# Attention in 36 slots and experts with gathers two jobs ahead: every engine put into written order

## The chip, the cores and the metric

The kernel runs on one core of one Trainium2 chip. The metric is the device time of one execution in microseconds (us), lower is better. A core has five engines with a queue each: TensorE (PE in the profile; its weight loads are PEld), VectorE (DVE), ScalarE (ACT), GpSimd (POOL) and SyncE (SP, which here only issues transfers). Each engine takes its own instructions in order and waits for others by semaphores.

## The reference

Eight batches, eight heads, 576 tokens, head dimension 64. Attention without softmax, an RMS norm per head, then a switch layer: each of the 4608 tokens goes to one of eight experts.

```python
kv  = einsum('bhsd,bhse->bhde', k, v)
o   = einsum('bhsd,bhde->bhse', q, kv)
o   = o / sqrt(mean(o*o, -1) + 1e-6) * g_norm
x   = o.transpose(0, 2, 1, 3).reshape(4608, 512)
logits = x @ w_gate                       # [4608, 8]
e   = argmax(logits, 1)
p   = softmax(logits)[n, e]
out = p * (relu(x @ w1[e]) @ w2[e])       # w1 [8,512,1024], w2 [8,1024,512]
```

All inputs are float32; the experts' weights and rows are used as float16.

## The kernel before

**Attention.** Four pairs of batches `P`, nine tiles of 128 tokens in each: four of the first batch, four of the second, and one with the last 64 tokens of both. `load_qkv` (L149) loads k, v or q of one batch into a 1 MB buffer `ld`, of which there are four; `load_q` copies q by heads into `qp` on POOL (L162). `kv_stage` (L174) forms k^T v of a batch: 80 matmuls into `kvp` (L187), copies to `kvs` (L194), transposes `kvtp` (L197), a copy `kvt` (L199), the product with the gate weights `kgp` (L202), a copy (L205). `x_tile` (L208) does one tile: transposes `qtp` (L212), copy `qts` (L214), `op` = q k^T v with the logits beside it (L219; two PSUM buffers), then the norm chain: `sq` on ACT (L230), `ms` on DVE (L235), `lnt` and `rinv` on ACT (L237, L239), the normalised rows `xg` and logits `lr` on DVE (L241, L247). `route` (L254) takes the tiles of a pair together (the last pair in four and five): `lg` and some fifteen small DVE instructions choose the expert, matmuls `pp` count ranks, and POOL scatters each tile's rows to `xs_scratch` in DRAM, sorted by expert (L305).

**Experts.** After counts and a table for left-over rows (L372 to L425), one job per expert plus one for rows beyond five tiles of an expert ("left", one tile here). A job gathers five tiles from `xs_scratch` on POOL (L496), transposes them (`xp`, L441, copy `xt`, L444), computes the row numbers `idx` (L446), `hp` = x w1 with a Relu copy `ht` on ACT (L462, L469), `yp` = h w2 (L478), scales to `ys` on DVE (L483), and POOL scatters to the output (L486). `load_w` loads w1 in float32 to the one buffer `wst` (SP, L127), scales it by g on POOL to `w1e` (L130), and loads w2 with a cast on POOL's queue (`w2e`, L133); four buffers of each.

**Order.** The program is traced as written, and the framework's scheduler then orders the instructions of each engine by its own costs; it may move work of one part between that of another. Only `issue_after` holds some scaling behind the scatters. In the expert loop the gathers of job n+1 are written ahead of `ffn_1` of job n.

Of the kernel before, what the change touches and what calls it, by code (L numbers as in the profile page):

```python
# [13 lines left out]
I32 = mybir.dt.int32  # L14
# [14 lines left out]
def kernel(  # L29
# [42 lines left out]
    for P in range(4):  # L72
# [44 lines left out]
        P_const.tile([128, RW], F16, tag=f"xe{n}", name=f"xe{n}") for n in range(2 * CT + 2)  # L117
# [4 lines left out]
    def load_w(e, after=None):  # L122
        e = e if isinstance(e, bass.DynSlice) else slice(e, e + 1)
        w1e = P_w.tile([128, 4, F], F16, tag="w1e", bufs=4, name="w1e")
        w2e = P_w.tile([128, 8, D], F16, tag="w2e", bufs=4, name="w2e")
        st = P_w.tile([128, 4, F], F32, tag="wst", bufs=1, name="wst")
        nc.sync.dma_start(st, moe_w1[e, :, :].rearrange("o (t p) f -> p (o t) f", p=128))  # L127
        with tc.issue_after(after) if after is not None else nullcontext():
            for kk in range(4):
                nc.gpsimd.tensor_scalar(  # L130
                    w1e[:, kk, :], st[:, kk, :], g2, 1.0, op0=ALU.mult, op1=ALU.mult
                )
            nc.gpsimd.dma_start(  # L133
                w2e, moe_w2[e, :, :].rearrange("o (t p) d -> p (o t) d", p=128)
            )
        return w1e, w2e

    weights = {}

    with (  # L140
        tc.tile_pool(name="pattn", bufs=1) as PA,
# [14 lines left out]
        def load_q(b):  # L156

            t = load_qkv(q, b)
            qp = PA.tile([128, 4, 8, 64], F32, tag="qp", bufs=2, name="qp")
            tv = t.rearrange("p h (j d) -> p h j d", j=4)  # L160
            for j in range(4):
                nc.gpsimd.tensor_copy(qp[:, j, :, :], tv[:, :, j, :])  # L162
            return qp

        def load_rem(src, b0, tag, bufs):
            t = PA.tile([128, 8, 64], F32, tag=tag, bufs=bufs, name=tag)
# [7 lines left out]
        def kv_stage(b, kb, vb, kr, vr):  # L174
            kvp = PSA.tile([128, 4, 64], F32, tag="kvp", bufs=1, name="kvp")
            r0 = 64 * (b % 2)
            for i in range(4):
                for j in range(5):
                    for hh in range(2):
                        h = 2 * i + hh  # L180
                        if j < 4:
                            lhs = kb[:, h, 64 * j:64 * j + 64]
                            rhs = vb[:, h, 64 * j:64 * j + 64]
                        else:
                            lhs = kr[r0:r0 + 64, h, :]
                            rhs = vr[r0:r0 + 64, h, :]
                        nc.tensor.matmul(  # L187
                            kvp[64 * hh:64 * hh + 64, i, :], lhs, rhs,
                            start=(j == 0), stop=(j == 4),
                        )  # L190
            kvs = kvs_bufs[b % 4]
            for hh in range(2):
                ps = slice(64 * hh, 64 * hh + 64)
                nc.vector.tensor_copy(kvs[ps, :, 64 * hh:64 * hh + 64], kvp[ps, :, :])  # L194
            kvtp = PSA.tile([128, 4, 128], F32, tag="misc", bufs=1, name="kvtp")
            for i in range(4):
                nc.tensor.transpose(kvtp[:, i, :], kvs[:, i, 0:128], ident)  # L197
            kvt = PA.tile([128, 4, 128], F32, tag="kvt", bufs=1, name="kvt")
            nc.scalar.copy(kvt, kvtp)  # L199
            kgp = PSA.tile([128, 4, 16], F32, tag="misc", bufs=1, name="kgp")  # L200
            for i in range(4):
                nc.tensor.matmul(  # L202
                    kgp[:, i, :], kvt[:, i, :], gw[:, i, :, :], start=True, stop=True
                )
            nc.vector.tensor_copy(kvs[:, :, 128:144], kgp)  # L205
            return kvs

        def x_tile(qsrc, parts, xg, lr, t):  # L208

            qtp = PSA.tile([128, 4, 128], F32, tag="qtp", bufs=2, name="qtp")  # L210
            for i in range(4):
                nc.tensor.transpose(qtp[:, i, :], qsrc(i), ident)  # L212
            qts = PA.tile([128, 4, 128], F32, tag="qts", bufs=2, name="qts")
            nc.scalar.copy(qts, qtp)  # L214
            op = PSA.tile([128, 2, 512], F32, tag="op", bufs=2, name="op")
            for i in range(4):
                c0 = (i % 2) * 144
                for c, kvs in parts:
                    nc.tensor.matmul(  # L219
                        op[c, i // 2, c0:c0 + 144],  # L220
                        qts[:, i, c],
                        kvs[:, i, :],
                        start=True,
                        stop=True,
                    )
            oc = op[:, :, 0:288].rearrange("p c (i n) -> p c i n", n=144)
# [9 lines left out]
            lnt = PA.tile([128, 8], F32, tag="lnt", bufs=3, name="lnt")  # L236
            nc.scalar.activation(lnt, ms, ACTF.Ln, scale=1.0 / 64.0, bias=epsb)  # L237
            rinv = PA.tile([128, 8], F32, tag="rinv", bufs=3, name="rinv")
            nc.scalar.activation(rinv, lnt, ACTF.Exp, scale=-0.5)  # L239
            r4 = rinv.rearrange("p (c i h) -> p c i h", c=2, i=2)  # L240
            nc.vector.tensor_tensor(  # L241
                xg[:, t, 0:512].rearrange("p (c i h n) -> p c i h n", c=2, i=2, h=2),
                ox,
                _bc(r4, 4, 64),
                op=ALU.mult,
            )
            nc.vector.tensor_tensor(  # L247
                lr[:, t, :, :].rearrange("p (c i h) n -> p c i h n", c=2, i=2),
                ol,
                _bc(r4, 4, 8),  # L250
                op=ALU.mult,
            )

        def route(g0, G, xg, lr, tile0):  # L254
            lg = PA.tile([128, G, 8], F32, tag="lg", bufs=2, name="lg")
            nc.vector.reduce_sum(lg, lr[:, g0:g0 + G, :, :].transpose([0, 1, 3, 2]), axis=AXX)
            mx = PA.tile([128, G], F32, tag="mx", bufs=2, name="mx")
            nc.vector.tensor_reduce(mx, lg, axis=AXX, op=ALU.max)
            dl = PA.tile([128, G, 8], F32, tag="dl", bufs=2, name="dl")
            nc.vector.tensor_tensor(dl, lg, _bc(mx, 2, 8), op=ALU.subtract)  # L260

            cd = PA.tile([128, G, 8], F32, tag="cd", bufs=2, name="cd")
            nc.vector.scalar_tensor_tensor(
                out=cd, in0=dl, scalar=0.0, in1=_bc(rev8, 1, G),
                op0=ALU.is_ge, op1=ALU.mult,
            )
            m2 = PA.tile([128, G], F32, tag="m2", bufs=2, name="m2")
            nc.vector.tensor_reduce(m2, cd, axis=AXX, op=ALU.max)
# [324 lines left out]
```

## Time and profile before

| | us |
|---|---|
| median of 3 runs | 422.68 (421.56 to 424.37) |
| the profiled execution | 424.92 |
| its span in the profile | 423.1 |
| busy in the span: PE, DVE, ACT, POOL | 299.4, 143.6, 118.5, 194.0 |
| first stage, to the last scatter of rows | 0 to 201 |
| experts, first `hp` to last `yp` | 213.4 to 413.9 |

The profile's page splits the span into 40 slices with the busy tenths of each engine; the trace can be asked for the busy time of any stretch, for groups of instructions by line, for the instructions in order of time, and for the chain of waits: the work that ended last, followed back from each step to what released it. "PEclk" is TensorE's granted clock as a share of 2.4 GHz.

### The profile page before, as it was taken

To read this page: it belongs to the slowest core of one execution; us is meant where nothing else is said; L and a number is where in the kernel's file an instruction comes from. 1 tells how busy PE (TensorE), PEld (TensorE's weight loads), DVE (VectorE), ACT (ScalarE), POOL (GpSimd) and SP (SyncE) were. 2 spreads that over 40 slices of the span, in tenths; PEclk is the share of its full clock that TensorE was granted. 3 is DMA by queue.
4 is the path that set the end of the run, shared out by engine and by line. 5 is a ranking of instruction groups with operands and counts; after the bars stand their busy time and mean duration, and the time that the engine had idled before them with its cause. 6 is when DMAs were issued, how large, how long until landed. Compare 5 with 4: busy or idle time off the path is not lost.

```text
span 423.1 us, 5972 instructions
## 1 busy us (share of the span) xinstructions
PE 299.4 (71%) x2278; PEld 211.3 (50%) x2278; DVE 143.6 (34%) x370; ACT 118.5 (28%) x294; POOL 194.0 (46%) x216
## 2 busy tenths in 40 slices
PE   0789777845695468740196958879598696979991
PEld 0587666744584457640063534545345354445750
DVE  0134645371246415458213304233141331313321
ACT  1034514430335014340041140422405014041520
POOL 7220238307640371524874673747646472543221
PEclk9999977985699658875586997989989699889997
DMA  8995989987999299151288586566776347231111
GB/s 229 254 308 132 242 305 325 233 223 198 335 281 231 78 324 248 50 200 50 64 246 225 194 156 237 143 153 254 131 267 144 63 138 124 76 108 75 42 52 67
DMA packets 59725, 76.20 MB, mean 180 GB/s; under 512 B 16429, under 2 KB 50478, under 8 KB 59696
## 3 DMA queue, kind: packets, MB, share of 16 engines
q1 hardware_dynamic: 43360, 47.42, 37.2%
q0 software_dynamic: 16336, 28.40, 27.5%
q8 instruction: 18, 0.29, 0.3%
q14 instruction: 11, 0.09, 0.1%
HBM read 71.70 MB, written 15.50 MB: 206 GB/s over the span
## 4 chain that ended last, share of the span: by engine, by line
PE 33%; issue 20%; DMA 16%; POOL 10%; DVE 8%; ACT 6%; SPq 2%; another core or an unknown queue 1%; POOLq 1%; DVEq 0%
PE op L219 11%; PE yp L478 7%; DMA xe<-xs_scratch,rowi 6%; DMA out_dram<-ys,idx 5%; PE kvp L187 5%; POOL out_dram L486 3%; POOL xe L496 3%; PE kgp L202 3%; PE hp L462 3%; ACT sq L230 2%; PE qtp L212 2%; DMA wst<-in_moe_w_dram 2%; POOL w1e L130 2%; ACT qts L214 2%; PE kvtp L197 2%
## 5 line engine op out<-in xcount | busy, mean ns | idle before, releaser
L469 ACT ACTIVATE ht<-hp 128x320 f16<-128x320 f32 (+1 forms) x136 | 56.5, 428 | 156.5 <-PE hp L462 91.4
L478 PE MATMUL yp<-w2e,ht 128*128 128x512 f16 x328 | 85.4, 413 | 0.0
L462 PE MATMUL hp<-xt,w1e 128*128 128x320 f16 (+1 forms) x544 | 77.6, 300 | 10.3 <-ACT ht L469 8.7
L486 POOL DMA_INDIRECT out_dram<-ys,idx x41 | 42.0, 1024 | 73.9 <-DVE ys L483 66.2
L305 POOL DMA_INDIRECT xs_scratch<-xg,sli x36 | 35.3, 981 | 79.4 <-DVE sli L303 57.3
L462 PEld LDWEIGHTS <-w1e 128*128 128x128 f16 x544 | 52.9, 99 | 34.9 <-issue 13.2
L219 PE MATMUL op<-kvs,qts 128*128 128x144 f32 (+1 forms) x320 | 51.8, 340 | 21.2 <-DVE lr L247 13.4
L219 PEld LDWEIGHTS op<-kvs,qts 128*128 128x128 f32 (+1 forms) x320 | 47.0, 222 | 25.1 <-ACT rinv L239 14.3
L478 PEld LDWEIGHTS <-ht 128*128 128x128 f16 x328 | 34.0, 106 | 38.6 <-issue 9.2
L130 POOL TENSOR_SCALAR w1e<-wst,g 128x1024 f16<-128x1024 f32 x36 | 39.8, 1116 | 19.1 <-issue 8.6
L496 POOL DMA_INDIRECT xe<-xs_scratch,rowi x40 | 41.1, 1027 | 12.1 <-issue 11.6
L441 PE MATMUL xp<-ch,xe 128*128 128x128 f16 x164 | 19.7, 267 | 37.8 <-DMA xe<-xs_scratch,rowi 19.5
L446 DVE SCALAR_TENSOR_TENSOR idx<-xe,valid,bigm 128x1 int32<-128x1 int32 x40 | 12.0, 305 | 98.2 <-DMA xe<-xs_scratch,rowi 95.3
L235 DVE TENSOR_REDUCE ms<-sq 128x8 f32<-128x512 f32 x36 | 24.7, 686 | 58.7 <-ACT sq L230 56.2
L483 DVE TENSOR_SCALAR ys<-yp,xe 128x512 f32<-128x512 f32 x41 | 30.7, 749 | 40.7 <-PE yp L478 39.6
L441 PEld LDWEIGHTS <-xe 128*128 128x128 f16 x164 | 14.9, 119 | 46.0 <-issue 23.4
L162 POOL COPY qp<-ld 128x512 f32<-128x512 f32 x32 | 18.3, 620 | 38.0 <-DMA ld<-in_q_dram 38.0
L230 ACT ACTIVATE sq<-op 128x512 f32<-128x512 f32 x36 | 21.5, 598 | 46.8 <-PE op L219 45.1
L187 PE MATMUL kvp<-ld 128*64 128x64 f32 x512 | 26.9, 256 | 10.5 <-DMA ld<-in_v_dram 10.5
L187 PEld LDWEIGHTS kvp<-ld 128*64 128x64 f32 x512 | 22.0, 163 | 13.6 <-issue 10.9
L214 ACT COPY qts<-qtp 128x512 f32<-128x512 f32 x36 | 20.8, 582 | 26.2 <-PE qtp L212 26.2
L212 PE MATMUL qtp<-cf,qp 128*128 128x128 f32 x128 | 21.4, 307 | 7.3 <-issue 6.6
(87 smaller groups left out, 213.3 us busy)
## 6 DMA issues: line engine op xcount, KB each, us to landing
wst<-in_moe_w_dram SPq DMA_DIRECT2D x9, 2048.0 KB, 12.2
w2e<-in_moe_w_dram POOLq DMA_DIRECT2D x9, 1024.0 KB
ld<-in_k_dram SPq DMA_DIRECT2D x8, 1024.0 KB, 7.6
ld<-in_v_dram SPq DMA_DIRECT2D x8, 1024.0 KB, 7.9
ld<-in_q_dram SPq DMA_DIRECT2D x8, 1024.0 KB, 11.0
kr<-in_k_dram SPq DMA_DIRECT2D x8, 128.0 KB, 9.6
vr<-in_v_dram SPq DMA_DIRECT2D x8, 128.0 KB, 7.2
qr<-in_q_dram SPq DMA_DIRECT2D x8, 128.0 KB, 9.8
```

What stands on the lines that cost most here:

```text
L130: nc.gpsimd.tensor_scalar(w1e[:, kk, :], st[:, kk, :], g2, 1.0, op0=ALU.mult, op1=ALU.mult)
L187: nc.tensor.matmul(kvp[64 * hh:64 * hh + 64, i, :], lhs, rhs, start=(j == 0), stop=(j == 4),)
L219: nc.tensor.matmul(op[c, i // 2, c0:c0 + 144], qts[:, i, c], kvs[:, i, :], start=True, stop=True,)
L230: nc.scalar.activation(sq.rearrange("p (c i h) n -> p c i (h n)", c=2, i=2), oc[:, :, :, 0:128], ACTF.Square,)
L305: sent = nc.gpsimd.indirect_dma_start(out=xs_views[tile0 + g0 + t], out_offset=IndirectOffsetOnAxis(ap=sli[:, t:t + 1], axis=0), in_=xg[:, ...
L441: nc.tensor.transpose(xp[:, c, :], xe[t][:, c * 128:(c + 1) * 128], ident16)
L462: nc.tensor.matmul(hp, w1e[:, kk, f * 128:(f + 1) * 128], xt[:, kk, ws * wd:(ws + 1) * wd], start=(kk == 0), stop=(kk == 3),)
L469: nc.scalar.activation(ht[:, f, ws * wd:(ws + 1) * wd], hp, ACTF.Relu)
L478: nc.tensor.matmul(yp, ht[:, f, t * 128:(t + 1) * 128], w2e[:, f, :], start=(f == 0), stop=(f == 7),)
L483: nc.vector.tensor_scalar(ys, yp, xe[t][:, 514:516].bitcast(F32), None, op0=ALU.mult)
L486: nc.gpsimd.indirect_dma_start(out=views[t], out_offset=IndirectOffsetOnAxis(ap=idx[:, t:t + 1], axis=0), in_=ys, in_offset=None, bounds_c ...
L496: nc.gpsimd.indirect_dma_start(out=xe.bitcast(I32), out_offset=None, in_=xs.ap(), in_offset=IndirectOffsetOnAxis(ap=rows, axis=0), bounds_ ...
```

## The change

Both stages are put under `tc.manual_schedule` with all five engines, so that each engine gets its instructions in the order in which they are written.

- Attention is 36 slots, one per tile. Slot s has `x_mm(s)` (`op`), `x_qt(s+2)` (transposes two tiles ahead), the norm chain, and lists of other work: `mid`, `late`, `last`. k^T v of the next batch is put in parts into the four or five slots ahead of its first tile; routing is split in `first`, `ranks` and `send`, in the last slot of a group and the one after it. The last pair is routed in 4, 3 and 2 tiles.
- `ld` has six buffers for four; a batch is loaded two batches ahead. `xe` has sixteen for twelve: three sets of five and one.
- Weights: three buffers each for four. W[0] and W[1] are scaled on POOL during attention, the other seven on VectorE inside the jobs. `stage` (w1 to `wst`) of W[n+3] is issued in job n after the scaling of W[n+2], `second` (w2) of W[n+3] at the end of job n.
- In job n the gathers of job n+2 are issued first; the transposes of job n+1 (`flip`) stand among the second half of the `hp` groups.

```diff
-            t = PA.tile([128, 8, 256], F32, tag="ld", bufs=4, name="ld")
+            t = PA.tile([128, 8, 256], F32, tag="ld", bufs=6, name="ld")
...
+        first_slot = [9 * (b // 2) + 4 * (b % 2) for b in range(B)]
+        for b in range(1, B):
+            f = first_slot[b]
+            n = 4 if b % 2 else 5
+            plan = [[0, 1], [2, 3]] if n == 4 else [[0], [1, 2], [3]]
+            for m, ii in enumerate(plan):
+                for i in ii:
+                    at(late, f - n + m, kv_mm, b, i)
+            at(last, f - 3, kv_copy, b)
+            at(late, f - 2, kv_t, b)
+            at(mid, f - 1, kv_gate, b)
+            for j in range(4):
+                at(last, f - 4 + j // 2, heads, b, j)
+            if b + 2 < B:
+                at(last, f - 2, load_batch, b + 2)
+        for P, g0, G in [(0, 0, 9), (1, 0, 9), (2, 0, 9), (3, 0, 4), (3, 4, 3)]:
+            rt = Route(P, g0, G)
+            s = 9 * P + g0 + G - 1
+            at(last, s, rt.first)
+            at(late, s + 1, rt.ranks)
+            at(last, s + 1, rt.send)
+        at(last, first_slot[4] - 2, W[0].stage)
+        at(last, first_slot[6] - 2, W[0].second)
+        for kk in range(4):
+            at(last, 23 + kk // 2, W[0].scale, nc.gpsimd, kk)
+        at(last, 25, W[1].stage)
+        for kk in range(4):
+            at(last, 32 + kk // 2, W[1].scale, nc.gpsimd, kk)
+        at(last, 33, W[2].stage)
...
+        load_batch(0)
...
+        for j in range(4):
+            heads(0, j)
+        for t in xe_bufs:
+            nc.gpsimd.memset(t, 0.0)
...
+        for s in range(36):
+            op = x_mm(s)
+            for fn in mid[s]:
+                fn()
+            if s + 2 < 36:
+                qt = x_qt(s + 2)
+            rest = x_norm(s, op)
+            if s + 2 < 36:
+                x_qs(s + 2, qt)
+            for fn in late[s]:
+                fn()
+            rest()
+            for fn in last[s]:
+                fn()
+        rt = Route(3, 7, 2)
+        rt.first()
+        rt.ranks()
+        rt.send()
...
+            rows(0)
+            W[1].second()
+            rows(1)
+            W[2].second()
+            for t in range(CT):
+                jobs[0].flip(t)
+            for n in range(len(order)):
+                job = jobs[n]
+                if n == 4:
+                    jobs[7] = left_over(0, 3 * CT, out_views[E * CT])
+                    W[7] = jobs[7].w
+                nxt = jobs[n + 1] if n + 1 < len(order) else None
+                rows(n + 2)
+                flips = list(range(nxt.nt)) if nxt is not None else []
+                for ws in range(job.halves):
+                    for f in range(8):
+                        job.one(ws, f)
+                        if ws == job.halves - 1 and f >= 2 and flips:
+                            nxt.flip(flips.pop(0))
+                        if ws == (n == 0) and f % 2 == 1 and n + 2 < len(order):
+                            W[n + 2].scale(nc.vector, f // 2)
+                            if f == 7 and n + 3 < len(order):
+                                W[n + 3].stage()
+                for t in range(job.nt):
+                    job.two(t)
+                if n + 3 < len(order):
+                    W[n + 3].second()
```

The functions that the slots and jobs call hold the instructions of before: `kv_mm`, `kv_copy`, `kv_t` and `kv_gate` are the parts of `kv_stage`, `one` and `two` those of `ffn_1` and `ffn_2`. `x_norm` issues `sq` and `ms` and returns `rest`, which issues `lnt`, `rinv`, `lr` and `xg`. In it `lr` now stands ahead of `xg`; in `Route`, `ex`, `se` and the two writes into `xg` move from `first` to `ranks`.

## Rows read from the trace of the kernel before

**Rows 1.** The page's 40 slices: tenths of the transfer engines' busy share.
```profile
DMA  8995989987999299151288586566776347231111
```

**Rows 2.** Busy time by stretch, attention: stretch, length, PE, PEld, DVE, ACT, POOL, clock, transfer share, GB/s.
```profile
0.00:114.00 114.00, 75.78 (x740) 66.10 (x741) 41.24 (x112) 33.97 (x84) 45.58 (x69) 0.87 0.92 252
100.00:125.00 25.00, 17.11 (x160) 15.42 (x161) 6.92 (x15) 8.35 (x20) 15.63 (x19) 0.73 1.08 306
```

**Rows 3.** Instructions in order of time at the seam: start, us, engine, line, operation.
```profile
191.23 0.72 DVE L256 TENSOR_REDUCE lg<-lr 128x40 f32<-128x320 f32 x1
...
213.39 9.99 PE L462 MATMUL hp<-xt,w1e 128*128 128x320 f16 x64
```

**Rows 4.** Busy time by stretch, two expert jobs (columns as in rows 2).
```profile
229.10:255.50 26.40, 20.86 (x126) 12.17 (x125) 6.75 (x15) 6.78 (x16) 15.74 (x15) 0.89 0.70 186
...
281.40:306.80 25.40, 19.98 (x123) 11.69 (x121) 6.64 (x14) 6.79 (x16) 16.10 (x16) 0.95 0.72 195
```

**Rows 5.** The chain of waits, at the seam and between two jobs: start, us, what.
```profile
200.41 2.53 DMA xs_scratch<-xg,sli
...
244.20 0.97 POOL w2e L133
...
246.84 7.54 DMA xe<-xs_scratch,rowi
...
255.15 0.59 PE xp L441 x4
```

**Rows 6.** Instructions in order of time, TensorE in the last job.
```profile
396.41 8.86 PE L462 MATMUL hp<-xt,w1e 128*128 128x320 f16 x64
...
405.11 8.80 PE L478 MATMUL yp<-w2e,ht 128*128 128x512 f16 x40
```

**Rows 7.** The chain of waits, TensorE's pieces in attention (x16: two tiles).
```profile
24.25 3.95 PE op L219 x16
...
74.99 1.02 PE qtp L212 x8
...
116.16 2.20 PE op L219 x16
118.36 3.53 PE kvp L187 x80
...
124.16 1.08 PE kgp L202 x8
```

**Rows 8.** Instructions in order of time, the norm chain of one tile alone.
```profile
50.51 0.60 ACT L230 ACTIVATE sq<-op 128x512 f32<-128x512 f32 x1 [1.54 <-PE op L219]
51.14 0.69 DVE L235 TENSOR_REDUCE ms<-sq 128x8 f32<-128x512 f32 x1 [1.28 <-ACT sq L230]
...
53.05 0.21 DVE L247 TENSOR_TENSOR lr<-op,rinv 128x64 f32<-128x64 f32 x1
```

**Rows 9.** Instructions in order of time: first and last of VectorE's routing of nine tiles.
```profile
91.82 1.18 DVE L256 TENSOR_REDUCE lg<-lr 128x72 f32<-128x576 f32 x1
...
95.72 0.17 DVE L303 CAST sli<-sl 128x9 int32<-128x9 f32 x1
```

**Rows 10.** Groups by line and form: count, busy us, mean ns, idle before them.
```profile
L194 DVE COPY kvs<-kvp 64x256 f32<-64x256 f32 x16 | 6.8, 422 | 14.8 <-PE kvp L187 8.6 <-remote 6.0
L391 DVE TENSOR_SCALAR thr<-cf 128x256 f32<-128x256 f32 x1 | 0.3, 286 | 0.0
...
L305 POOL DMA_INDIRECT xs_scratch<-xg,sli x36 | 35.3, 981 | 79.4 <-DVE sli L303 57.3 <-DVE bigm L380 12.7 <-issue 8.8
```

**Rows 11.** Instructions in order of time: `idx` beside a scaling and beside a gather's issue.
```profile
211.29 1.13 POOL L130 TENSOR_SCALAR w1e<-wst,g 128x1024 f16<-128x1024 f32 x1
211.68 0.76 DVE L446 SCALAR_TENSOR_TENSOR idx<-xe,valid,bigm 128x1 int32<-128x1 int32 x1 [0.62 <-DMA xe<-xs_scratch,rowi]
...
237.87 1.02 POOL L496 DMA_INDIRECT xe<-xs_scratch,rowi  x1 [0.30 <-issue]
238.06 0.22 DVE L446 SCALAR_TENSOR_TENSOR idx<-xe,valid,bigm 128x1 int32<-128x1 int32 x1 [1.02 <-DMA xe<-xs_scratch,rowi]
```

More of the change, by code (lines that the diff above doesn't have):

```diff
@@ L116, with __init__, stage, scale @@
     xe_bufs = [
-        P_const.tile([128, RW], F16, tag=f"xe{n}", name=f"xe{n}") for n in range(2 * CT + 2)
+        P_const.tile([128, RW], F16, tag=f"xe{n}", name=f"xe{n}") for n in range(3 * CT + 1)
     ]
     tabi = P_const.tile([128, 2, 32], I32, tag="tabi")
[L122 to L132, printed above, removed]
+    class Weights:
+        def __init__(self, e):
+            self.e = e if isinstance(e, bass.DynSlice) else slice(e, e + 1)
+        def stage(self):
+            self.st = P_w.tile([128, 4, F], F32, tag="wst", bufs=1, name="wst")
+            nc.sync.dma_start(
+                self.st, moe_w1[self.e, :, :].rearrange("o (t p) f -> p (o t) f", p=128)
+            )
+        def scale(self, eng, kk):
+            if kk == 0:
+                self.w1 = P_w.tile([128, 4, F], F16, tag="w1e", bufs=3, name="w1e")
+            eng.tensor_scalar(
+                self.w1[:, kk, :], self.st[:, kk, :], g2, 1.0, op0=ALU.mult, op1=ALU.mult
+            )
+        def second(self):
+            self.w2 = P_w.tile([128, 8, D], F16, tag="w2e", bufs=3, name="w2e")
             nc.gpsimd.dma_start(
-                w2e, moe_w2[e, :, :].rearrange("o (t p) d -> p (o t) d", p=128)
+                self.w2, moe_w2[self.e, :, :].rearrange("o (t p) d -> p (o t) d", p=128)
             )
-        return w1e, w2e
-    weights = {}
+    ENG = mybir.EngineType
+    by_hand = {ENG.PE, ENG.Activation, ENG.DVE, ENG.Pool, ENG.SP}
+    order = list(range(E - 1)) + ["left", E - 1]
+    W = [Weights(e) if e != "left" else None for e in order]
     with (
+        tc.manual_schedule(engines=by_hand),
         tc.tile_pool(name="pattn", bufs=1) as PA,
@@ L154, in load_qkv, with load_rem @@
             return t
[L156 to L166, printed above, removed]
+        def load_rem(src, b0, tag):
+            t = PA.tile([128, 8, 64], F32, tag=tag, bufs=2, name=tag)
             for bb in range(2):
@@ L172, in load_rem @@
             return t
-        def kv_stage(b, kb, vb, kr, vr):
-            kvp = PSA.tile([128, 4, 64], F32, tag="kvp", bufs=1, name="kvp")
-            r0 = 64 * (b % 2)
[L177 to L191, printed above, removed]
+        ld, rem, qp, kvst = {}, {}, {}, {}
@@ new lines, with at @@
+        first_slot = [9 * (b // 2) + 4 * (b % 2) for b in range(B)]
+        mid = {s: [] for s in range(-4, 36)}
+        late = {s: [] for s in range(-4, 36)}
+        last = {s: [] for s in range(-4, 36)}
+        def at(where, s, fn, *args):
+            where[s].append(lambda: fn(*args))
+        for b in range(1, B):
[12 more added lines that the diff above has]
+                at(last, f - 2, load_batch, b + 2)
@@ L522, in left_over_load @@
             )
-            return [gather(xe_bufs[t0], gi)], w, okm, bgm
-        def load_x(e):
-            return [
-                gather(xe_bufs[(e % 2) * CT + t], rowi[:, e, t:t + 1])
-                for t in range(CT)
-            ]
-        def job(e):
-            if e == "left":
-                xe, w, okm, bgm = left
-                return xe, w, okm, bgm, [out_views[E * CT]]
-            return (rows[e], weights[e], valid[:, e, :], bigm[:, e, :],
-                    out_views[e * CT:(e + 1) * CT])
@@ L560 @@
             with tc.For_i(1, nov) as t:
-                xe, w, okm, bgm = left_over_load(t, 2 * CT + 1)
-                xt, idx = ffn_x(xe, okm, bgm)
-                ht = ffn_1(xt, 1, w[0])
-                ffn_2(xe, ht, idx, w[1], [out_views[E * CT + 1]])
+                job = left_over(t, 3 * CT, out_views[E * CT + 1])
+                job.w.stage()
+                for kk in range(4):
+                    job.w.scale(nc.vector, kk)
+                job.w.second()
+                job.flip(0)
+                for f in range(8):
+                    job.one(0, f)
+                job.two(0)
 _INS = ['q', 'k', 'v', 'g_norm', 'moe_w_gate', 'moe_w1', 'moe_w2']
```

568 lines of the change are left out of this document (305 added, 263 removed).

## The prediction

> **What bounds the kernel now.** I read the slices of the page first, then the busy time by stretch, then the chain of waits in each stage.
>
> The slices (10.6 us each) show the transfers busy at 0.7 or more in 14 of the first 16, at 0.1 to 0.5 in the four after them, then mostly at 0.5 to 0.8 up to the 30th [rows 1]. The first stage, attention and routing, moved 252 GB/s over its first 114 us at a transfer share of 0.92, while TensorE was busy for 75.8 of these 114 us [rows 2]. So attention runs near its transfers, and TensorE is not its bound: its mean granted clock there is 0.87, from 100 to 125 only 0.73, which means that part of it runs at 1.2 GHz.
>
> Between attention and experts lies a seam: from the last `lg` at 191.23 to the first `hp` at 213.39 are 22.2 us [rows 3].
>
> In the expert stage a job of five tiles takes some 26 us, with TensorE busy for 20 to 21 of them at a clock of 0.89 to 0.95 [rows 4]. The chain shows why: the last gather for the next job is issued behind `w2e` on POOL's queue and lands 7.54 us after its issue; then the transposes start from idle, and `xp` takes 0.59 us a tile [rows 5]. The last job, which waits for no gather, takes 17.5 us from its first `hp` to the end of its last `yp` [rows 6].
>
> **The change, stage by stage.** *Start.* The loads of batch 0 keep their order on SP, so the first `op` stays at 24 us [rows 7]. Six `ld` buffers in place of four let batch 1 be issued whole; the clearing of 16 `xe` buffers moves behind the first `heads` copies, where POOL has nothing due. Cost 0.
>
> *Slots 0 to 26.* TensorE at full clock, per tile: `op` 2.20/2 = 1.10 and `qtp` 1.02/2 = 0.51, so 1.61; per batch: `kvp` 3.53, `kgp` 1.08 and `kvtp`, four transposes as in `qtp`, 0.51, so 5.12 [rows 7]. Nine tiles with two batches: 9 x 1.61 + 2 x 5.12 = 24.7 us. VectorE with ScalarE: from the start of `ms` to the end of `lr` 51.14 to 53.26 = 2.12 us, with `lnt` and `rinv` of ScalarE between; the next `sq` fits under `xg` and `lr` [rows 8]. Routing nine tiles takes 91.82 to 95.89 = 4.1 us of VectorE [rows 9], the copies of a batch 2 x 0.42 and a smaller one, about 1.1 [rows 10]. Nine slots: 9 x 2.12 + 4.1 + 2 x 1.1 = 25.4 us. The two sums are nearly equal, but their peaks fall into different slots, and every engine is now in order. On TensorE a slot with two of the four `kvp` parts takes 1.61 + 1.77 = 3.4 (two such, beside the one that shares with `ranks`), with one part 2.5 (two), with `kvtp` 2.1 (two), with `kgp` 2.7; on VectorE the slot of `first` takes 2.12 + 2.5 = 4.6, that of `ranks` and `send` 4.0. The larger in each slot, over nine: 4.6 + 4.0 + 2 x 3.4 + 2 x 2.5 + 2 x 2.1 + 2.7 = 27.3; with waits between engines I take 28. Then 27 slots end at 24 + 3 x 28 = 108 us.
>
> Transfers up to k and v of batch 7: seven batches of 3.54 MB, 2.36 MB of the last, 2.1 MB of W[0] and 2.4 MB of scatters = 31.7 MB. At the old rate of 252 GB/s that is 126 us, at 306, the best 25 us stretch, 104 [rows 2]. I take 252/0.92 = 274 GB/s, thus 116 us, since with six buffers a batch is always queued. `kvp` stands ahead of the next tile on TensorE, so a late k or v stops it. Behind the nine scatters of `send` on POOL, 9 x (0.98 + some 0.30 between) = 11.5 us [rows 10], stand the `heads` copies 2 and 3 of the next batch; they are due four slots, some 12 us, later. For such waits 3 us: slot 27 starts at 119.
>
> *Slots 27 to 35.* No next batch after slot 30, but two more routing parts of 3.3 to 4.1 us. The larger in each slot: 4.0 + 3.4 + 2.1 + 4.0 + 3.8 + 2.1 + 4.0 + 3.7 + 2.1 = 29 us. The last tile is normalised at 148.
>
> *Seam.* Two tiles are left to route: 3.3 us of VectorE (4.1 less 0.8 of the shorter `lg`), 0.3, two scatters 1.3 apart, 2.5 until the second lands, five gathers 5.2 to the last issue, 2.5 to land, 0.6 to `hp` = 15.7, say 16 for 22.2 [rows 3, 5]. The left-over table, some 25 instructions of VectorE of at most 0.29 [rows 10], so up to 7 us, hides under scatters and gathers; without that cover it is added. First `hp` at 164.
>
> *Experts.* A job at full clock is 17.5 plus five tiles of transposes, between 5 x 0.59/2 = 1.5 and nothing (they overlap `hp`); I take 1.2: 18.7 us. Gathers two jobs ahead are issued some 18 us before they are read, which covers the 7.54. What is late next is transfers: 0.70 x 26.4 = 18.5 and 0.72 x 25.4 = 18.3 us of them per job [rows 4], 98% of 18.7. There is one `wst`, so `stage` of W[n+3] waits for the scalings of W[n+2]; these stand ahead of the flips on VectorE, so a late `wst` stops `xt` and `ys` and through them TensorE. I allow 1.1 us in jobs 1 to 5, and 3 us in job 0, whose flips read rows gathered behind W[1].second. Scaling moves from POOL to VectorE for seven weights. The trace has no such instruction: it takes at least 0.29, the row of 256 columns, and at most four times that, 1.15 [rows 10]; I take 0.7. Four add 2.8 us (1.2 to 4.6) to VectorE's 6.8 of 26.4 [rows 4]: hidden. Sum: 21.7 + 5 x 19.8 + 18.7 + 4 (left: eight `yp`, 32 short `hp`) + 17.5 = 161. Bounds: 150 without the allowances, and 178 with 22.4 us in jobs 0 to 5 (18.4 us of transfers at a share of 0.82, midway between 0.72 and 0.92).
>
> *Port.* `idx` takes 0.22 us while POOL issues a gather, but took 0.76 while POOL scaled `w1e`, and ended with it at 212.4 [rows 11]: the two engines can shut each other out, and the issue of a gather did not do so. By these rows the scaling on VectorE costs nothing on the path. The Trainium skill (SBUF — State Buffer, section "SBUF: two separate sides") goes further: a VectorE instruction in a two-port mode and a GpSimd one exclude each other for their whole length, and GpSimd cannot write the descriptors of its DMAs meanwhile. The trace agrees with the lock; no row here shows it on descriptors.
>
> *Tail.* From the end of the last `yp`, 413.9, to the end of the span 9.2 us [rows 6]; they stay.
>
> **Sum.** 24 + 95 + 29 + 16 + 161 + 9.2 = 334.2 us of span, where before has 423.1. The profiled execution's own time is 1.8 us above its span, 424.9, so 336.0; the median of the runs shown, 422.7, is 2.2 below that execution. I predict 334.
>
> **The rivals.**
> 1. *Attention keeps its old transfer rate.* For it: a share of 0.92 leaves little to fill. Against: after slice 16 the transfers are half idle while attention still computes [rows 1]. Slot 27 at 129: 344.
> 2. *Experts bound by transfers*, 22.4 us a job, as two more `w2e` fall into the first jobs. For it: 18.4 us of transfers per job. Against: stretches above 0.9 exist [rows 2]. 334 + 17 = 351.
> 3. *The attention order changes nothing*: its bound is elsewhere, and the trace has `kvp` between tiles now. Only seam and jobs gain: 213.4 - 6 + 161 + 9.2 - 0.4 = 377.
> 4. *The written order serialises a slot*, each waiting for the end of the one before: 1.61 + 0.60 for `sq` [rows 8] + 2.12 + 5.12/4.5 + 4.1/9 = 5.9 us, 36 slots 214, `hp` at 254, in all 424; with TensorE at half clock 2.7 more a slot, 521. I put it at 470; it decides from 5.9 us a slot. Against: transposes are written two slots ahead, and `op` has two buffers. This is the side slower than before.
> 5. *The port holds up both engines*: each of 28 scalings waits for an issue of 1.0 us or makes one wait, none hidden: 334 + 28 = 362. For it the 0.76, against it the 0.22. It is what the page above would do here.
>
> **How the numbers follow.** Forecast 0.60, rivals 1 to 5: 0.15, 0.13, 0.06, 0.03, 0.03. All bounds at their low end (compute's 108 hides the 104; 27 for the last slots) give 24 + 84 + 27 + 16 + 150 + 9.2 - 0.4 = 310, rivals 1 and 2 together 361. The forecast's own range is half way to these, 322 to 347. The range from 314 to 360 leaves out rivals 3, 4 and most of 5, and some 0.06 beside. Faster by over 1%, about what a measurement of this kernel can tell: 0.96, all but rival 4 and 0.01 for causes I do not see; slower by over 1%: 0.02; within 1%: 0.02.
>
> **What would show it.** First `op` near 24, slot 27 near 119, first `hp` near 164 and jobs near 19.8 show the terms right one by one; a clock of 1.0 through the experts shows that the gaps are gone. TensorE waiting for `ld` before slot 27 is rival 1; VectorE waiting for `wst` rival 2; POOL issues above 1.03 us beside a scaling rival 5; slots near 6 us rival 4. The prediction is wrong if slots are bound by a wait that I priced at 0.7 us per nine slots, as ScalarE's copy of `kvt` in the middle of a norm chain, or if shares near 1 don't last.

## The result and the profile after

The changed kernel takes 350.95 us (median of 4 runs, 348.39 to 352.36), the kernel before 422.74 beside it: a ratio of 0.829, 95% interval 0.824 to 0.835. The profiled execution took 351.07 us with a span of 349.3, where the kernel before has 423.1. Some kernels below also ran in a slower state, over 1.5% above their fastest run; ratios are those of the faster runs alone.

The profile page's slices come first: clock and transfers, 8.7 us to a slice.

```profile
PEclk9999999859996999675559999999998999999996
DMA  7999999994999772017179879698696969793021
```

Transfers are at 0.9 or more in most of the first 13 slices, where [rows 1] already had 0.8 and 0.9. What is new stands behind them: from the 21st to the 36th slice transfers are at 0.6 to 0.9, in seven of the sixteen at 0.9, where before they went along at 0.5 to 0.8 and lower, and the clock is at 0.9 or more from the 22nd slice on, but for one slice and the last. The same stretches as in [rows 2], and two expert jobs as in [rows 4] (columns as there):

```profile
0.00:114.00 114.00, 84.24 (x942) 73.67 (x942) 49.19 (x126) 44.11 (x107) 46.77 (x75) 0.93 1.00 290
100.00:125.00 25.00, 20.37 (x216) 17.50 (x217) 11.62 (x25) 11.35 (x29) 15.43 (x19) 0.86 0.96 318
191.53:211.50 19.97, 19.43 (x129) 11.69 (x128) 11.45 (x25) 7.81 (x19) 9.60 (x10) 1.00 0.86 236
228.00:247.00 19.00, 18.39 (x124) 11.09 (x121) 8.15 (x17) 6.99 (x16) 9.61 (x11) 1.00 0.88 258
```

In these two jobs TensorE is now busy for 97% of the time at full clock, where [rows 4] had 79% at 0.89 to 0.95. In the attention it is busy for 84 of 114 us, where [rows 2] had 76. The milestones, in order of time (start, us, engine, line, operation): slot 27, the last `lg`, the first `hp`, the fifth and sixth job's `hp`, the last `yp`.

```profile
127.13 1.22 PE L281 MATMUL op<-kvs,qts 128*128 128x144 f32 x8
...
162.21 0.37 DVE L329 TENSOR_REDUCE lg<-lr 128x16 f32<-128x128 f32 x1
...
178.72 8.35 PE L590 MATMUL hp<-xt,w1e 128*128 128x320 f16 x44
...
258.55 6.14 PE L590 MATMUL hp<-xt,w1e 128*128 128x320 f16 x44
...
281.17 6.14 PE L590 MATMUL hp<-xt,w1e 128*128 128x320 f16 x44
...
331.93 8.80 PE L604 MATMUL yp<-w2e,ht 128*128 128x512 f16 x40
```

Against [rows 3] and [rows 6] the 73.8 us of span divide like this: up to the last `lg` 191.23 - 162.21 = 29.0; the seam, last `lg` to first `hp`, 22.2 - 16.5 = 5.7; the experts, first `hp` to the end of the last `yp`, 200.5 - 162.0 = 38.5; the tail 0.6. Against the forecast:

| term | forecast | profile after | late by |
|---|---|---|---|
| slot 27 starts | 119 | 127.1 | 8.1 |
| slots 27 to 35 (last tile) | 29 (148) | 35.1 (162.2) | 6.1 |
| seam | 16 | 16.5 | 0.5 |
| experts | 161 | 162.0 | 1.0 |
| tail | 9.2 | 8.6 | -0.6 |

So 14.2 of the 15.1 us of span that the forecast misses lie in the attention. Two losses are plain in the trace. The first is a stretch in which ScalarE and VectorE sit idle although the results they need of TensorE have long been there. Instructions in order of time; `[..]` is the idle time before one and what ended it ("remote": nothing that the profile knows):

```profile
60.95 1.15 PE L281 MATMUL op<-kvs,qts 128*128 128x144 f32 x8
...
64.47 1.07 PE L241 MATMUL kgp<-gw,kvt 128*128 128x16 f32 x8 [2.38 <-issue]
...
65.39 0.63 PE L263 MATMUL qtp<-cf,qp 128*128 128x128 f32 x4
...
68.10 0.60 ACT L297 ACTIVATE sq<-op 128x512 f32<-128x512 f32 x1 [3.24 <-remote]
...
70.99 0.23 DVE L244 COPY kvs<-kgp 128x64 f32<-128x64 f32 x1 [5.28 <-remote]
...
71.27 2.29 PE L281 MATMUL op<-kvs,qts 128*128 128x144 f32 x8 [5.25 <-DVE kvs L244]
```

`kgp` is complete at 65.5 and its copy starts at 70.99. The same comes at 104.6 (3.43 us idle before it) and 137.5 (2.07). All three begin inside a closed series of nine scatters on GpSimd, issued one behind another (57.9 to 69.1, 96.0 to 107.1, 130.3 to 141.4). Behind the third, TensorE also waits 2.94 us for `qp`. The second loss is this pair, at the end of attention:

```profile
151.49 4.84 DVE L335 TENSOR_TENSOR dl<-lg,mx 128x24 f32<-128x24 f32 x1
...
151.90 4.41 POOL L135 TENSOR_SCALAR w1e<-wst,g 128x1024 f16<-128x1024 f32 x4
...
157.12 0.18 PE L355 MATMUL pp<-cs,ch 128*128 128x24 f16 x1 [6.94 <-DVE cs L347]
```

A subtraction of 24 columns, which takes 0.17 to 0.48 us in the other parts, takes 4.84 us and ends at 156.33, as GpSimd's four scalings of W[1] end at 156.31.

### The profile page after: what moved, and what is told of

It is laid out like the page before. It is cut to its first block, busy times and chain, and to the rows that moved or that the text cites. A ratio compares the mean times of both kernels' runs of the same rounds, so it can differ in the third digit from the quotient of the medians.

```text
span 349.3 us, 5957 instructions
## 1 busy us (share of the span) xinstructions
PE 272.6 (78%) x2279; PEld 195.1 (56%) x2279; DVE 165.0 (47%) x414; ACT 121.7 (35%) x295; POOL 164.6 (47%) x192
## 4 chain that ended last, share of the span: by engine, by line
PE 26%; DMA 26%; DVE 13%; POOL 12%; issue 12%; SPq 4%; another core or an unknown queue 2%; ACT 2%; POOLq 1%; DVEq 0%
DMA w2e<-in_moe_w_dram 12%; DMA out_dram<-ys,idx 9%; PE hp L590 7%; PE yp L604 7%; POOL xs_scratch L389 5%; PE op L281 5%; DMA ld<-in_v_dram 3%; PE kvp L219 3%; POOL xe L543 2%; POOL out_dram L612 2%; SPq L170 2%; DVE xg L314 2%; DVE ms L302 2%; PE qtp L263 2%
## 5 line engine op out<-in xcount | busy, mean ns | idle before, releaser
L590 PE MATMUL hp<-xt,w1e 128*128 128x320 f16 (+1 forms) x544 | 82.0, 302 | 1.2 <-ACT ht L597 1.2
L604 PE MATMUL yp<-w2e,ht 128*128 128x512 f16 x328 | 72.3, 379 | 0.0
L590 PEld LDWEIGHTS <-w1e 128*128 128x128 f16 x544 | 52.3, 100 | 21.3 <-issue 1.3
L281 PE MATMUL op<-kvs,qts 128*128 128x144 f32 (+1 forms) x320 | 50.8, 327 | 12.1 <-DVE kvs L244 7.6
L604 PEld LDWEIGHTS <-ht 128*128 128x128 f16 x328 | 32.1, 98 | 37.1
L281 PEld LDWEIGHTS op<-kvs,qts 128*128 128x128 f32 (+1 forms) x320 | 42.6, 203 | 15.2 <-DVE kvs L244 8.2
L200 POOL COPY qp<-ld 128x512 f32<-128x512 f32 x32 | 18.4, 614 | 42.8 <-DMA ld<-in_q_dram 42.8
L297 ACT ACTIVATE sq<-op 128x512 f32<-128x512 f32 x36 | 21.5, 596 | 35.7 <-PE op L281 23.7
L219 PE MATMUL kvp<-ld 128*64 128x64 f32 x512 | 24.5, 245 | 10.6 <-DMA ld<-in_v_dram 10.6
L571 PE MATMUL xp<-ch,xe 128*128 128x128 f16 x164 | 17.5, 235 | 16.0 <-DMA xe<-xs_scratch,rowi 10.0
L219 PEld LDWEIGHTS kvp<-ld 128*64 128x64 f32 x512 | 19.9, 153 | 15.0 <-issue 13.9
L574 DVE COPY xt<-xp 128x512 f16<-128x512 f16 x41 | 17.2, 418 | 18.9 <-PE xp L571 16.3
L571 PEld LDWEIGHTS <-xe 128*128 128x128 f16 x164 | 13.1, 105 | 20.8 <-DMA xe<-xs_scratch,rowi 11.6
L314 DVE TENSOR_TENSOR xg<-op,rinv 128x512 f16<-128x512 f32 x36 | 24.5, 682 | 0.2
```

Source lines behind the costliest of these rows:

```text
L219: nc.tensor.matmul(kvp[64 * hh:64 * hh + 64, i, :], lhs, rhs, start=(j == 0), stop=(j == 4),)
L281: nc.tensor.matmul(op[c, i // 2, c0:c0 + 144], qts[s][:, i, c], kvs[:, i, :], start=True, stop=True,)
L314: nc.vector.tensor_tensor(xg[:, r, 0:512].rearrange("p (c i h n) -> p c i h n", c=2, i=2, h=2), ox, _bc(r4, 4, 64), op=ALU.mult,)
L571: nc.tensor.transpose(xp[:, c, :], xe[t][:, c * 128:(c + 1) * 128], ident16)
L590: nc.tensor.matmul(hp, self.w.w1[:, kk, f * 128:(f + 1) * 128], self.xt[:, kk, ws * wd:(ws + 1) * wd], start=(kk == 0), stop=(kk == 3),)
L604: nc.tensor.matmul(yp, self.ht[:, f, t * 128:(t + 1) * 128], self.w.w2[:, f, :], start=(f == 0), stop=(f == 7),)
```

## The experiments

Each kernel is the changed one with the edit shown. They ran on three chips (experiments 1 to 4, then 5, 6, 7 and 9, then 8, 10, 11 and 12), each beside the kernel before, so ratios to it are compared, and medians only on one chip.

**1. The q copies ahead of the scatters.**

```
-                at(last, f - 4 + j // 2, heads, b, j)
+                at(last, f - 4 + (j // 2 if b % 2 == 0 else 0), heads, b, j)
```

> The four q copies of an odd batch are all written ahead of the nine scatters of the part before, instead of two ahead and two behind. Theory (GpSimd's written order delays the copies): the 2.94 us that TensorE waits for qp at 142 us goes, and so does the 0.6 us at 107.7, since the copies no longer stand behind 11.4 us of scatters; time 347 us, first hp 3 to 4 us earlier. Rival (the wait only shows what something else would hold): the 142 us wait turns into another wait of the same length, 350 to 351 us. The idle stretches of VectorE before the copy of the gated k^T v at 65.7, 101 and 135 us should stay under both.

Measured: one run of 347.29 us and three of 353.4 to 354.2, before 425.09. They spread too far to say whether the edit gains. In the profile, of a run of 353.38 us, the wait for `qp` behind the scatters is gone, the unexplained stretches are not: 2.44 us before the copy of `kgp` at 67.97, 3.79 before `kvs` at 97.88, 0.85 to 2.25 before three instructions of ScalarE. Slot 27 starts at 129.05 and the last `lg` comes at 163.22, no earlier than in the changed kernel's profile; experiment 2, whose order is unchanged up to there, starts slot 27 at 132.77. As it stands this speaks for the rival; experiment 10 takes it up again.

**2. W[1] scaled by VectorE.**

```
-            at(last, 32 + kk // 2, W[1].scale, nc.gpsimd, kk)
+            at(last, 28 + kk, W[1].scale, nc.vector, kk)
```

> The scaling of W[1] (4 times 1.1 us on GpSimd at 151.9 to 156.3 us) is made by VectorE, one piece per slot in slots 28 to 31. Theory (the 4.84 us subtraction dl at 151.49 us was held by the shared port, since its end falls on the end of GpSimd's scaling): dl takes 0.2 us, TensorE's wait of 6.9 us at 157 us shrinks to about 2, and VectorE pays 4 times 0.74 us in slots where it has 8 us of slack: 346 to 347 us. Rival (dl was held by something else, or the part's end is set by the norm chain): dl stays above 3 us or the time stays within 1 us of 351.

Measured: a ratio of 0.813 (0.804 to 0.821), below the changed kernel's 0.829. The subtraction, in order of time, and VectorE's own scaling:

```profile
151.59 0.75 DVE L135 TENSOR_SCALAR w1e<-wst,g 128x1024 f16<-128x1024 f32 x1
...
157.35 0.18 DVE L335 TENSOR_TENSOR dl<-lg,mx 128x24 f32<-128x24 f32 x1
```

0.18 us for 4.84, and TensorE's wait behind it is 2.58 us for 6.94. From the `lg` of the four-tile part to the last `lg` it takes 18.3 us for 21.5. The lock is shown, at some 3 to 5 us. This profiled execution as a whole, 351.03 us, is no shorter than the changed kernel's: the ranks of slot 27 are 5.6 us later (132.49 for 126.84), behind unexplained stretches.

**3. The routing parts later.** Ranks and scatters of P = 0 and 1 four slots later.

```
-            at(late, s + 1, rt.ranks)
-            at(last, s + 1, rt.send)
+            d = 5 if P < 2 else 1
+            at(late, s + d, rt.ranks)
+            at(last, s + d, rt.send)
```

> Ranks and scatters of the parts of P=0 and P=1 are put four slots later (slots 13 and 22 instead of 9 and 18); the part of P=2 stays, as a control in the same run. Theory (results of TensorE reach ScalarE and VectorE late while GpSimd's scatters run and the batch's k^T v is gated): the idle stretches at 62 to 71 and 101 to 107 us go, the one at 135 to 139 stays; 341 to 345 us, or, if the scatters then hold the even batch's gating at slots 17 and 26 instead, 349 to 351 with the idle stretches moved there. Rival (the stall belongs to the odd batch's gating, or to the loads around it): the idle stretches stay where they are in the sequence of slots, 350 to 352 us.

Measured: a ratio of 0.840 (0.834 to 0.846). The stretches moved with the scatters (now 70.0 to 81.2 and 106.4 to 117.5), and beside one of them stands a wait with a plain cause:

```profile
81.22 4.49 POOL L200 COPY qp<-ld 128x512 f32<-128x512 f32 x8
...
81.91 1.11 PE L263 MATMUL qtp<-cf,qp 128*128 128x128 f32 x4 [7.44 <-POOL qp L200]
...
82.89 0.60 ACT L297 ACTIVATE sq<-op 128x512 f32<-128x512 f32 x1 [8.21 <-remote]
```

TensorE stands 7.44 us for a q copy that GpSimd makes behind its series, this time for the even batch. The loss belongs to the series, not to the odd batch's gating; whether to its length or to what it stands in front of is still open.

**4. Weights loaded later.**

```
-        at(last, first_slot[6] - 2, W[0].second)
+        at(last, 27, W[0].second)
...
-        at(last, 25, W[1].stage)
+        at(last, 27, W[1].stage)
```

> The load of the first expert's second weights (slot 25) and of the second expert's first weights (slot 25) are issued behind slot 27, when the last q, k and v are on their way. Theory A (engines, not transfers, set the slots up to 27): nothing, 350 to 352 us, slot 27 at 127. Rival B (transfers set them): 4 MB less ahead of slot 27 would let it start up to 8 us earlier, 343 to 346 us. A loss, 352 to 356, would say that the first expert then waits for its second weights.

Measured: a ratio of 0.836 (0.828 to 0.844), slot 27 at 131.94. Lightening the transfers by two loads makes it start no earlier. In the changed kernel's own profile TensorE waits for k and v for 0.4 us between its first `op` and slot 27. Transfers don't set the pace; the forecast's first rival falls here too.

**5. and 6. The scatters spread, one to a slot.**

```
-            at(last, s + 1, rt.send)
+            if P < 3:
+                at(last, s + 1, rt.place)
+                for t in range(G):
+                    at(last, s + 1 + t * 7 // 8, rt.one, t)
+            else:
+                at(last, s + 1, rt.send)
```

`place` works out the rows, `one` sends one tile; the sixth experiment adds the edit of the second.

> The nine scatters of each of the first three parts are written one per slot (slots 9 to 16, 18 to 25, 27 to 34) instead of one behind another in one slot. In all six traces so far nearly every unexplained idle stretch of ScalarE and VectorE in the attention lies inside a series of scatters, always at an instruction that needs a result of TensorE, and it moved when the series was moved. Theory S (a closed series of scatters on GpSimd delays what TensorE reports to ScalarE and VectorE): with the series broken up the stretches above 2 us vanish, nine slots take 31 to 32 us in all three cycles, slot 27 starts near 118 and the time is 338 to 343 us. Rival (each scatter costs its share of delay wherever it stands): the stretches become some eight small ones per cycle with about the same sum, 349 to 353 us. Second rival (the delay has to do with the gating and the odd batch alone): they stay at slots 10 to 13, 349 to 353.

> The spread scatters together with the scaling of W[1] on VectorE. If both theories hold the gains add: 3 to 5 us (port lock on dl) below the run with the spread scatters alone, 334 to 339 us. If the lock's 4.8 us were only cover for something else the two runs are alike within 1 us.

Measured: 332.39 us (0.795, 0.790 to 0.800) and 328.33 us (0.785, 0.780 to 0.791), before 418.1. Slot 27 starts at 110.96 in the fifth, 16 us earlier than in the changed kernel, and the last `lg` at 145.06. The sixth is 4.1 us faster than the fifth on the same chip. In the fifth `dl` is not held (0.18 us), but two other small instructions of the same part are, each while GpSimd makes two scalings (137.02 to 139.24 and 140.47 to 142.68):

```profile
137.02 2.24 DVE L366 TENSOR_TENSOR csum<-csum,tsum 128x8 f32<-128x8 f32 x1
...
140.46 2.25 DVE L388 TENSOR_TENSOR t<-t,oh 128x24 f32<-128x24 f32 x1
```

In the sixth they take 0.17 and 0.18 us: the lock once more. No unexplained stretch is left in either. But that alone proves nothing, as the next run shows.

**7. Rows one job ahead.**

```
             rows(0)
             W[1].second()
-            rows(1)
...
-                rows(n + 2)
+                rows(n + 1)
```

> Expert rows are gathered one job ahead instead of two. Prediction's view (the rows of a job came 7.5 us after its gather in the kernel before and stood on the chain): one job ahead is 20 us, so the flips, which start 11 us into a job, would find their rows in most jobs; 350 to 353 us. Rival (the second job of lead is what took the wait for rows away): TensorE waits 1 to 3 us for xe in each of seven jobs, 358 to 370 us.

Measured: 425.46 us, a ratio of 1.016 (1.010 to 1.023): all of the change's gain is gone. TensorE waits 71 us for rows, up to 13.4 us in a job. Waits (engine, line, what for: us in total, times, longest), then the transfers issued from 196 to 224 us (queue, count, median us to landing):

```profile
PE xp L571 <- DMA xe<-xs_scratch,rowi: 71.0, 10, 13.4
```

```profile
w2e<-in_moe_w_dram POOLq DMA_DIRECT2D x1, 1024.0 KB, 14.4
...
xe<-xs_scratch,rowi POOLq DMA_INDIRECT x5, 12.1
```

The rows stand behind the 1 MB of second weights and land with them. The rival named the right wait, but put it at 1 to 3 us a job.

The attention of this run is that of the changed kernel, and here the loss shows itself without any unexplained stretch:

```profile
60.37 1.14 POOL L389 DMA_INDIRECT xs_scratch<-xg,sli  x1 [6.02 <-DVE sli L387]
...
70.66 0.96 POOL L389 DMA_INDIRECT xs_scratch<-xg,sli  x1 [0.30 <-issue]
71.61 3.38 POOL L200 COPY qp<-ld 128x512 f32<-128x512 f32 x6
```

```profile
60.76 1.25 PE L281 MATMUL op<-kvs,qts 128*128 128x144 f32 x8
...
65.73 1.25 PE L281 MATMUL op<-kvs,qts 128*128 128x144 f32 x8
72.30 1.11 PE L263 MATMUL qtp<-cf,qp 128*128 128x128 f32 x4 [5.32 <-POOL qp L200]
...
107.11 1.11 PE L263 MATMUL qtp<-cf,qp 128*128 128x128 f32 x4 [5.15 <-POOL qp L200]
...
141.66 1.11 PE L263 MATMUL qtp<-cf,qp 128*128 128x128 f32 x4 [5.20 <-POOL qp L200]
```

The two `op` at the top begin slots 11 and 13. In each of three cycles TensorE stands some 5.2 us for a copy that GpSimd makes behind nine scatters, 15.7 us in all, two of the three ahead of slot 27 (which starts at 126.68) and one behind. The last `lg` comes at 160.96, about where the changed kernel's profile has it.

**8. Rows one job ahead, but ahead of the weights.** As the seventh, with the gathers at the end of the job before the load of second weights.

```
                 for t in range(job.nt):
                     job.two(t)
+                rows(n + 2)
                 if n + 3 < len(order):
                     W[n + 3].second()
```

> Rows one job ahead, as in the run of 425 us, but the five gathers stand ahead of the load of the second weights on GpSimd's list, not behind it. Theory (rows came 8 to 14 us after their issue because the 1 MB of weights issued just ahead of them was in their queue): rows land 3 to 6 us after their issue, TensorE's wait in a job falls from 13.4 to 2 to 5 us, time 355 to 380 us. Rival (they are late because GpSimd comes to them only after the job's five output scatters): the wait shrinks by the 1.3 us of the weights' issue alone, 413 to 420 us.

Measured: 383.33 us, a ratio of 0.913 (0.908 to 0.918). From 196 to 220 us, and the waits of the experts:

```profile
w2e<-in_moe_w_dram POOLq DMA_DIRECT2D x1, 1024.0 KB, 10.2
...
xe<-xs_scratch,rowi POOLq DMA_INDIRECT x5, 5.6
```

```profile
PE xp L571 <- DMA xe<-xs_scratch,rowi: 29.3, 12, 4.5
```

Rows land after 5.6 us for 12.1, and by the two ratios 43 of the 78 us that experiment 7 lost come back from the place in the queue alone. The theory holds, though the time is just above the end of what it expected. The other 35 us, again by the ratios, are what the second job of lead is still worth: with one, TensorE waits 29.3 us for rows, and its clock is lower (0.876 for 0.909 over the span).

**9. The attention's order left to the scheduler.**

```
-        tc.manual_schedule(engines=by_hand),
         tc.tile_pool(name="pattn", bufs=1) as PA,
```

> The same instructions, but the attention's order is left to the scheduler; the experts stay in written order. Theory (the attention's and the seam's gain, about 35 of the 74 us, come from the order): 375 to 390 us, first hp at 200 to 215. Rival (it comes from more buffers, the batch spread in parts and the smaller routing parts, whatever the order): 345 to 358 us.

Measured: 364.16 us, a ratio of 0.869 (0.864 to 0.874), between the two expectations. Its waits of TensorE up to 200 us:

```profile
PE qtp L262 <- POOL qp L199: 18.8, 4, 6.4
...
PE op L280 <- DVE xg L313: 7.3, 6, 2.2
```

The first `hp` comes at 198.55. Against 0.829 times the 418.1 us of the kernel before on this chip, 346.7 us, the attention's written order is worth 17 us; the rest of the gain is there without it. The same wait for `qp` behind scatters stands here too, 6.4 and 6.3 us in two of the four.

**10. and 11. The first and the fifth experiment again, on one chip.** The unexplained stretches stand in the profiles of the changed kernel and of experiments 1 to 4, and in none of the experiments on the second chip. The seventh kernel has the attention of the changed one and none of them, so the first experiment was repeated.

> The kernel with the odd batch's q copies ahead of the scatters once more, beside the spread scatters on one chip. In the run with rows one job ahead, whose attention is that of the changed kernel, TensorE stood 5.3, 5.2 and 5.2 us for qp at 72, 107 and 142 us while GpSimd made its nine scatters, and no stretch was unexplained. Theory B (the copies' place behind the scatters is the loss): without unexplained stretches this edit alone gives what spreading gives, ratio 0.795 to 0.805. Theory S (a closed series of scatters delays TensorE's reports): unexplained stretches of 2 to 5 us lie in the three series again, and the ratio stays at 0.825 to 0.835.

> The spread scatters once more, on the same chip as the run above. Both theories: ratio 0.79 to 0.80 and no unexplained stretch above 2 us in slots 9 to 35; if the run above shows such stretches and this one does not, they come from the closed series; if both show them, theory S falls.

Measured: the copies ahead of the scatters 325.46 us, a ratio of 0.773 (0.768 to 0.779); the spread scatters 331.54 us, 0.789 (0.784 to 0.795); before 419.92. The first, in order of time:

```profile
112.06 2.19 PE L281 MATMUL op<-kvs,qts 128*128 128x144 f32 x8
...
143.21 0.37 DVE L329 TENSOR_REDUCE lg<-lr 128x16 f32<-128x128 f32 x1
...
159.78 7.89 PE L590 MATMUL hp<-xt,w1e 128*128 128x320 f16 x44
```

One line of the order, and the last `lg` comes 17.2 us earlier than with the unchanged attention on this chip (160.46 in experiment 8, 160.42 in experiment 12). No stretch is unexplained, though the series are closed: theory B holds, with more gain than it expected, and a closed series doesn't delay TensorE's reports by itself. This is the fastest kernel of the study. It still pays the lock (its `dl` takes 4.15 us); with the edit of experiment 2 as well it wasn't run. Spreading is the lesser cure: its scatters run into the last routing parts, whose first `lg` comes at 128.19 for 123.29.

**12. The experts' weights scaled by GpSimd.**

```
-                            W[n + 2].scale(nc.vector, f // 2)
+                            W[n + 2].scale(nc.gpsimd, f // 2)
```

> In the experts the four scalings of a job's weights are made by GpSimd (1.1 us each) instead of VectorE (0.74 us each), as in the kernel before. Prediction's view (they cost GpSimd 4.4 us of a job in which it has 20 less some 13, and hold VectorE's small two-operand instructions by the port): within 1.5 us of the changed kernel, ratio 0.825 to 0.84. Rival (GpSimd's scalings stand between a job's outputs and the next rows and hold VectorE): 1 to 3 us per job, ratio 0.85 to 0.88.

Measured: a ratio of 0.855 (0.848 to 0.862). First `hp` to last `yp` takes 174.7 us, for 162.0 in the changed kernel and 156.0 in experiment 10 on this chip: 1.8 to 2.7 us more in each of seven jobs, the rival. Its waits in the experts, and below it the changed kernel's:

```profile
DVE ys L609 <- DMA out_dram<-ys,idx: 58.1, 7, 12.9
```

```profile
DVE ys L609 <- DMA out_dram<-ys,idx: 17.3, 4, 5.1
```

GpSimd's four scalings (211.71 to 216.11 in one job) and five gathers stand ahead of the outputs of a job whose first `yp` began at 206.44; the first of these leaves at 216.29, and with four `ys` buffers VectorE waits for the outputs to leave, and TensorE for VectorE.

## Why the prediction was right, and where it was not

The time came out 17 us above the forecast and inside its range, and the mechanism was the forecast's: attention denser, seam shorter, jobs near 20 us. Two terms were mis-sized, in opposite directions, so that part of the nearness is luck. One bound is mis-added as well: without its allowances the experts' sum gives 152, not 150.

**Start, seam, tail: right.** First `op` 22.8 for 24, seam 16.5 for 16, tail 8.6 for 9.2.

**Experts: right.** The first six jobs, from `hp` to `hp`, take 21.3, 19.1, 19.6, 19.8, 22.6 and 18.4 us, together 120.9; the forecast had 21.7 + 5 x 19.8 = 120.7. The fifth is 2.8 us above its term, and the others make up for it. The whole stage, 162.0 us here, takes 156.0 to 158.0 in experiments 5, 6, 10 and 11, whose jobs are the same; why is not shown. The clock is 1.0 in both job windows above. VectorE's scaling takes 0.74 to 0.75 us alone and 0.81 on the average of 28, where the forecast took 0.7 out of 0.29 to 1.15. Transfers at a share of 0.86 and 0.88 don't stop TensorE: rival 2 falls. What the sum didn't show is how much rests on the two jobs of lead: experiment 7 prices it at 78 us. The 7.54 us of [rows 5] held a load queued ahead, and with rows one job ahead and jobs shorter it would have been 12.

**Slots 0 to 27: the term for waits was mis-sized.** The step said that copies 2 and 3 "are due four slots, some 12 us, later", and gave 3 us "for such waits". The queue was named rightly, and so were the four slots: the scatters are written in slot 9, and the transposes of slot 13 read the third copy. What it left out is that the series does not start in its own slot. It waits for `sli`, VectorE's last step of the routing, and TensorE runs ahead of that: in experiment 7 the first scatter starts at 60.37, when TensorE is about to begin slot 11 (60.76), and TensorE comes to the third copy at 66.98, 6.6 us later and not 12. The series takes 11.2 us, so each such wait costs 5.2. Two of them lie ahead of slot 27, and without them it starts at 112.06 for 126.16 (experiments 10 and 8, one chip). That is 14.1 us; what goes beyond the two waits goes with the clock, which is 0.90 of full speed in both of these cycles with the wait and 0.94 and 1.00 without. Nine slots then take 27.9 us (from 56.38 to 84.27, between two `pp`), for which the forecast had 28. That the loss on these chips is this wait, and not a slot's compute or the loads, experiments 7, 10 and 11 show.

For the changed kernel's own profile this is not shown to the end. There the unexplained stretches lie over the wait: TensorE waits less than 1 us for `qp` ahead of slot 27, and on the chip of experiment 1, where such stretches stood too, slot 27 starts at 129.05 without the wait and at 132.77 with it (experiment 2): 3.7 us apart, not 14.1. Either loss makes the attention about as long; which of them set these 8.1 us stays open.

**Transfers: mis-sized the other way.** 274 GB/s and 116 us were taken; without the wait (experiment 10) the kernel moves 301 GB/s over its first 111 us at a share of 1.05, TensorE waits 1.9 us for k and v behind its first `op`, and slot 27 starts at 112.06:

```profile
0.00:111.00 111.00, 89.51 (x1054) 78.88 (x1056) 57.69 (x145) 50.24 (x123) 48.60 (x76) 0.98 1.05 301
```

The two errors partly hide each other: the forecast's 119 lies between 112.06 without the wait and 127.1 with it. The bound "at 306" was nearly it, and rival 1, the other bound, is far off.

**Slots 27 to 35: a lock that was priced at nothing.** Of the 6.1 us some 3 to 4.6 are the subtraction held by GpSimd's scalings (3.2 by experiment 2, and 4.84 less 0.2); most of the rest is the third wait for `qp`, 2.94 us. The forecast had seen the lock in [rows 11], but asked only what scaling on VectorE would do, not what the scalings left on GpSimd would do to VectorE on the path. The Trainium skill (SBUF — State Buffer, section "SBUF: two separate sides") says that a VectorE instruction with two inputs in SBUF and a GpSimd one that reads SBUF exclude each other for a whole instruction. The trace agrees, and shows more: `dl` was held for the four scalings behind one another, not for one of 1.1 us. For GpSimd's descriptors the trace shows little of it: of the 82 issues of gathers and outputs, the 12 that overlap a scaling on VectorE take 1.14 us on average and at most 1.24, the other 70 take 1.00. The sign of rival 5, issues above 1.03 us, is there, but at a fraction of the 1.0 us that it priced, and the jobs take what the forecast had without it. Rival 5 falls.

**Rivals 3 and 4.** Attention gained 29 us, and slots take 3.9 us on average, far from 5.9. Part of rival 3 is true: the first `hp` moved forward by 34.7 us, and with the attention left to the scheduler 14.8 of these remain (213.39 to 198.55).

**"ScalarE's copy of kvt mid-chain"** was named as what would make the prediction wrong; in the profile of after there is a stretch of 0.87 us before it at 63.84, and it is one of the unexplained ones. It was not the cause.

## What to carry to other kernels

In a written order every engine's list is a queue: before a series of n issues goes into it, ask which instruction behind them is due first, and count the time to that from where the series can start, not from where it is written. A gather should stand ahead of a large load in the same queue, or far enough ahead in time not to care. Work on GpSimd that has no due time belongs where VectorE has no small two-operand instruction on the path.

## What the runs showed of the hardware

- Idle stretches of ScalarE and VectorE that nothing in the profile explains, each at an instruction that needs a result of TensorE, 0.8 to 8.2 us long. In the attention of five profiles (the changed kernel, experiments 1 to 4) all but two of 0.85 us began within a series of scatters, and in experiment 3 they moved with it; the profile before has one of 5.97 us, also beside scatters. In the eight later profiles, on two chips other than that of experiments 1 to 4, there are none; four of the eight kernels have the same closed series in the same order of the attention or nearly so. The same kernel took 347.3 to 354.2 us in experiment 1 and 322.6 to 326.2 in experiment 10. Of the 27 us between the two profiled spans (351.5 and 324.3) 17 lie between slots 9 and 27 (72.6 us between their `pp` there, 55.4 here), 3 in slots 27 to 35 and 7 in the experts. What delays TensorE's results there stays open; no run settled it.
- The loss by the `qp` wait and the unexplained stretches don't add: with either the last `lg` comes at 160 to 163 us (167 in experiment 4). Where the stretches were present (experiment 1), it came no earlier without the wait (163.22) than in the changed kernel's profile (162.21).
- A small subtraction on VectorE was held 4.84 and 4.15 us by four queued scalings on GpSimd (the changed kernel, experiment 10), and two other small instructions 2.24 and 2.25 us by two scalings each (experiment 5).
- Five gathers landed 12.1 us after their issue behind 1 MB of weights in the same queue, and 5.6 us ahead of it.
